# Exponent scaling of weight pieces on VectorE, shorter scratch stores, and the first small weight sums moved into the first GEMM

## The chip, the cores and the metric

The kernel runs on one core of a Trainium2 chip. The time is the device time of one execution in microseconds (us); before the change the median of four runs is 647.11 us (645.83 to 647.81). The engines are named as in the profile: PE is TensorE (PEld its weight loads), DVE is VectorE, ACT is ScalarE, POOL is GpSimd, and SP is SyncE, whose queue issues every DMA of this kernel.

## What is computed

A retention layer is followed by a two-layer network with ELU. All tensors are fp32; the weights reach the kernel as float64.

```python
# q, k, v: (4, 8, 768, 64);  w_in: (512, 2048);  w_out: (2048, 512)
gamma = 1.0 - 2.0 ** (-5.0 - np.arange(H))
for t in range(S):
    state = gamma * state + einsum('bhd,bhe->bhde', k[:, :, t], v[:, :, t])
    y[:, :, t] = scale * einsum('bhd,bhde->bhe', q[:, :, t], state)
x = y.transpose(0, 2, 1, 3).reshape(3072, 512)
h = x @ w_in
g = np.where(h > 0, h, np.exp(np.minimum(h, 0)) - 1)
out = g @ w_out
```

## The kernel before

The 3072 tokens are worked through in six blocks of 512. For each block the retention gives x (in chunks of 128 tokens), the first GEMM gives h, ELU gives g, and the second GEMM gives the output. From the second block on the GEMMs use Strassen's scheme, from there on partly twice nested. It replaces one of eight block products by sums of blocks of the weights and of the inputs. The sums of the weights are made once, in the first two blocks, and most of them are stored in DRAM (scratch, scratch2, scratch3) and fetched again later through a ring of buffers. The change lies in block 0 and in the making of these sums.

**Pieces.** The weights come as float64 in 16 pieces of 1 MB: pieces 0 to 7 are w_in, 8 to 15 w_out. `load_piece` (L136) loads one into one of three staging buffers (tile wraw). `prepare` runs three ScalarE operations on it: the low words scaled (L157), the exponent's top byte (L159), and the high words scaled by 2^-112 (L160). `decode` then runs two VectorE operations, a shift with a mask (L179) and an integer add (L182), which give the fp32 weights. Behind them it issues the load of the piece three further on, into the buffer just freed, and, for a piece of w_out, a store of the decoded blocks to scratch (L186). SP's queue is in order, so a load that waits for a decode holds up the DMAs behind it.

**Block 0, first GEMM (`plain_first`).** It is a plain product of 16 tiles (n = 0 to 15 in the loop at the end of the listing); a tile with 512 columns takes TensorE 3.4 us (L473). After each tile `elu` puts two activations on ScalarE (L440, L441) and one operation on VectorE (L444), which is put off to the next tile. Only L444 frees the tile's PSUM bank, and four banks go round. Between the tiles the loop emits other work by hand: loads of q, k, v for block 1 (`load`), their scaling on GpSimd (`scale_v`, L268), pieces (`next_piece`), and at n = 10 to 14 the retention of block 1: score products (L294) with masks on VectorE (L305), state products (L325) with state sums (L337), and the products of the outputs (L363, L389) with the copies `seen` (L377) and the scaling (L398). These products share four PSUM banks, in turn, so that each group of products needs the VectorE operations of the one before it to have read its bank.

**Block 0, second GEMM (`second_of_first`).** It has eight steps of seven products (L561), 6 us each. A step needs one decoded piece of w_out, four sums of its blocks (`sums_of_pieces`, L513, tile so), and four sums of the activations (`inputs_of_first`, L492). In its loop the kernel also makes the small sums, those of the nested scheme: `small_of_pieces` runs four operations on pieces of w_out and four on the sums (L597, in `combine_w_out`). Its results lie in xb (the x of block 0) and in gq["T3"] (named gT by the profile) until `send_small` stores them to scratch2 (L593). At the end the step's last products are added up on VectorE (`kept_sum`, L545), which frees the banks that the next GEMM begins with. `combine_x_parts(1)` (L417) writes the sums of block 1's x into xb.

**Block 1, first GEMM (`first`).** `combine_w_in` (L623) makes the sums of w_in. `combine_small` (L764) makes two nested sets of w_in on GpSimd, four operations each, near the end of this GEMM, and stores them to scratch3. Then the staging buffers are given up and the ring of fetched weights starts in their place.

The order on every engine is the order in which this program emits its instructions; each engine runs its own in order.

Of the kernel before, what the change touches and what calls it, by code (L numbers as in the profile page):

```python
# [9 lines left out]
FP32 = mybir.dt.float32  # L10
# [3 lines left out]
AF = mybir.ActivationFunctionType  # L14
# [4 lines left out]
def kernel(  # L19
# [119 lines left out]

    def prepare(parts=1):

        n = len(prepared)
        if n >= NPIECE:
            return
        t = staged[n]
        if n < 2 * NQ:
            dst = (w_a, w_b)[n % 2][n // 2].rearrange("p a b c d -> p (a b c d)")
        else:  # L150

            dst = w_s[n % NQ].rearrange("p a b c d -> p (a b c d)")[:, 0:1024]
        todo = []
        for part in range(parts):
            c = slice(part * 1024 // parts, (part + 1) * 1024 // parts)
            lo, hi, flat = t[:, c, 0], t[:, c, 1], dst.bitcast(U32)[:, c]
            nc.scalar.activation(flat, lo, AF.Copy, scale=2.0**-29)  # L157
            top = dst.bitcast(F8).rearrange("p (c b) -> p c b", b=4)[:, c, 3]
            nc.scalar.activation(top, hi.bitcast(FP32), AF.Copy, scale=2.0**-120, saturate=False)  # L159
            nc.scalar.activation(lo.bitcast(FP32), hi.bitcast(FP32), AF.Abs, scale=2.0**-112)  # L160
            todo.append((lo, flat))
        prepared.append((dst, todo))


# [1 line left out]


    quarters = lambda f: scratch.rearrange("(s k) p (f c) -> k f p s c", k=2, f=4)[f // 4, f % 4]

    def decode(fine=False):  # L170

        n = len(decoded)
        if n >= NPIECE:
            return
        dst, todo = prepared[n]
        decoded.append(dst.rearrange("p (a b) -> p a b", a=2))
        vec = nc.vector
        for c, flat in todo:
            vec.tensor_scalar(c, c, 3, 0x7FFFFFF8, ALU.logical_shift_left, ALU.bitwise_and)  # L179
            if fine:  # L180
                yield
            vec.tensor_tensor(out=flat, in0=c, in1=flat, op=ALU.add)  # L182
            yield
        load_piece()
        if n >= 2 * NQ:
            nc.sync.dma_start(quarters(ORDER_F[n - 2 * NQ])[:, 0:8], dst.rearrange("p (s c) -> p s c", c=P))  # L186

    def decode_all():
        for _ in decode():
            pass  # L190
# [316 lines left out]
    def sums_of_pieces(n):  # L507

        odd = n // 2 % 2
        t = so_[:, :, 3:7] if odd else so_[:, :, 0:4]  # L510
        both = w_s_.rearrange("p n j a b c -> p n (j a b c)")[:, n % NQ : n % NQ + 2, 0:1024]
        a21, a11, a12, a22 = (both[:, :, 256 * d : 256 * d + 256] for d in range(4))
        tt = lambda o, x, y, op: nc.vector.tensor_tensor(out=o, in0=x, in1=y, op=op)  # L513
        s4, s1, s2, s3 = (t[:, :, k] for k in range(4))
        tt(s1, a21, a22, ALU.add)
        tt(s2, s1, a11, ALU.subtract)
        for x in range(2):
            sums[n + x] = t[:, x]
        if odd:
            tt(s3, a11, a21, ALU.subtract)  # L520
            yield
            tt(s4, a12, s2, ALU.subtract)
        else:
            tt(s4, a12, s2, ALU.subtract)
            yield
            tt(s3, a11, a21, ALU.subtract)
        for x in range(2):
            nc.sync.dma_start(quarters(ORDER_F[n + x])[:, 8:16], sums[n + x].rearrange("p a (d c) -> p (a d) c", c=P))

    def small_of_pieces(at):  # L530

# [59 lines left out]
    def send_small():  # L591
        while to_send:
            nc.sync.dma_start(*to_send.pop(0))  # L593

    def combine_w_out(at, low, high):

        tt = lambda o, x, y, op: nc.vector.tensor_tensor(out=o, in0=x, in1=y, op=op)  # L597
        if at < 3:

            ms = [xb[:, k].rearrange("p (b c) -> p b c", c=P)[:, 0:3] for k in range(4)]  # L600
            ss = gq["T3"].rearrange("p (k f) (b c) -> p k (f b) c", k=4, c=P)
        else:
            ms, ss = (stage.tile([P, 4, 4, P], FP32, name="wi", tag="stage") for _ in range(2))
            ms = [ms[:, k, 0:3] for k in range(4)]
        ss = [ss[:, k] for k in range(4)]
        for first, dst, k in [(0, ms, 0), (3, ss, 1)][:: 1 if at < 3 else -1]:
            a11, a21, a12, a22 = (x[k][:, :, P * d : P * d + P] for x in (low, high) for d in range(2))
            s1, s2, s3, s4 = dst
            tt(s1, a21, a22, ALU.add)
            yield  # L610
            tt(s2, s1, a11, ALU.subtract)
            yield
            tt(s3, a11, a21, ALU.subtract)
            yield
            tt(s4, a12, s2, ALU.subtract)
            to = scratch2[first : first + dst[0].shape[1]].rearrange("j p (k f c) -> k f p j c", k=4, f=4)
            for k in range(4):
                to_send.append((to[k, at], dst[k]))
            yield
# [136 lines left out]

    W_IN = {2: w_a_[:, :, :, 1], 3: w_s_[:, :, 2]}

    def combine_small(j):

        t = stage.tile([P, 4, 4, P], FP32, name="wi", tag="stage")
        a11, a12, a21, a22 = (W_IN[j][:, 2 * r : 2 * r + 2, :, c, :] for r in range(2) for c in range(2))
        s1, s2, s3, s4 = (t[:, k].rearrange("p (n f) c -> p n f c", f=2) for k in range(4))
        tt = lambda o, x, y, op: nc.gpsimd.tensor_tensor(out=o, in0=x, in1=y, op=op)  # L764
        tt(s1, a21, a22, ALU.add)
        tt(s2, s1, a11, ALU.subtract)
        tt(s3, a11, a21, ALU.subtract)
        tt(s4, a12, s2, ALU.subtract)
        to_send.append((scratch3[j - 1], t.rearrange("p k f d -> p (k f d)")))
# [333 lines left out]
    def run(steps):  # L1103
        for _ in steps:
            pass

    def next_piece():
        decode_all()
        prepare()

    hslot = lambda: hpool.tile([P, 2, TH], FP32, name="h", tag="h")
    mslot = lambda: mpool.tile([P, 2, TH], FP32, name="m", tag="m")

    for n, _ in enumerate(inner):
        if n in (0, 2, 4, 6):
            load(CPB + n // 2)
        if n in (1, 3, 5, 7, 9):
            next_piece()
        if n in (3, 5, 7, 9):
            scale_v(CPB + (n - 3) // 2)  # L1120
        if n == 7:
            run(inputs_of_first(0, [hslot() for _ in range(3)]))
        elif n == 10:
            scores(1, 0)
            scores(1, 1)
        elif n == 11:
            decode_all()
            states(1, 0)
            states(1, 1)
            prepare()  # L1130
        elif n == 12:
            parts = inputs_of_first(4, [mslot() for _ in range(3)])
            next(parts)
            outputs_step(1, 0)
            prepare()
        elif n == 13:
            decode_all()
            outputs_step(1, 1)
            prepare()
            run(parts)  # L1140
        elif n == 14:
            decode_all()
            parts = sums_of_pieces(0)
            next(parts)
            outputs_step(1, 2)
        elif n == 15:
            run(parts)
            decode_all()

    for n in second_of_first():  # L1150
        send_small()
        if n == 0:
            run(small_of_pieces(0))
            prepare()
            parts = sums_of_pieces(2)
            next(parts)
        elif n == 1:
            run(parts)
            run(small_of_pieces(1))
            next_piece()  # L1160
        elif n == 2:
            next_piece()
            parts = sums_of_pieces(4)
            next(parts)
        elif n == 3:
            run(inputs_of_first(2, [hslot(), hslot(), mslot()]))
            run(parts)
            next_piece()
        elif n == 4:
            run(inputs_of_first(6, [hslot(), mslot(), hslot()]))  # L1170
            decode_all()
            parts = sums_of_pieces(6)
            next(parts)
        elif n == 5:
            run(small_of_pieces(2))
            run(parts)
        elif n == 6:
            run(combine_w_in(0))
            send_small()
            xparts = combine_x_parts(1)  # L1180
            next(xparts)
            next(xparts)
            held["last"] = small_of_pieces(3)
            for _ in itertools.islice(held["last"], 3):
                pass
    run(xparts)

    ring = tpool = None
# [17 lines left out]
    sides = [  # L1206
        itertools.chain(combine_w_in(1), last), itertools.chain(combine_w_in(2), combine_w_in(3)), iter(()), iter(()),
    ]
    smalls = [], [], [3], [2]
    for n in range(NQ):  # L1210
        load(2 * CPB + n)
        cur = first(n)
# [185 lines left out]
```

## Time and profile before

| What | us |
|---|---|
| median of the runs | 647.11 |
| profiled execution, its own time | 644.94 |
| its span (first to last instruction) | 642.9 |
| TensorE busy in the span | 628.4 |
| VectorE busy | 479.5 |
| ScalarE busy | 258.9 |
| GpSimd busy | 38.5 |
| block 0, first GEMM, from its first tile on | 17 to 87 |
| block 0, second GEMM | 87 to 138 |
| block 1, first GEMM | 142 to 194 |

The span is what the instructions cover; the execution's own time is 2.0 us longer. A line of the timeline gives the start, the length (for several instructions, that of all of them together), engine, line, operation, what is written and read, shapes and count, and in brackets how long the engine had been idle before it and what ended that. A line of the waits gives who waited for whom, the sum in us, the times, and the longest.

### The profile page before, as it was taken

Reading aid. Unit: us, or ns where it says so; the run is one execution under the profiler, and the core shown is the slowest. Engines: PE = TensorE matmul, PEld = TensorE weight load, DVE = VectorE, ACT = ScalarE, POOL = GpSimd, SP = SyncE. Lnnn points to the kernel's source line nnn. Section 1 sums busy time; section 2 is a strip of 40 time slices with the busy share of each in tenths; the row PEclk is TensorE's granted clock in tenths of the full one; section 3 lists DMA queues with packets and bytes.
Section 4 is the critical chain, followed back from the end, with each engine's and each line's share of the span. In section 5 each row is a group of like instructions: output and inputs, shape, how many; then the busy total and the mean of one; then the engine's idle time right before and its main releaser. Section 6 shows DMA issues by size and latency. Waiting matters only on the chain.

```text
span 642.9 us, 16071 instructions
## 1 busy us (share of the span) xinstructions
PE 628.4 (98%) x6622; PEld 561.5 (87%) x6622; DVE 479.5 (75%) x858; ACT 258.9 (40%) x480; POOL 38.5 (6%) x41
## 2 busy tenths in 40 slices
PE   7999999879999999999999999999999999999998
PEld 4764578768888999989999989999988999988997
DVE  5648797977978776589777488867578959557976
ACT  6789744204452112546111465211465311356311
POOL 1011000000450000100000110000020000000000
PEclk9999999999999999999999999999999999999999
DMA  8697699979387789802889821788840688710794
GB/s 308 283 325 273 200 274 275 317 218 244 142 273 241 237 253 319 282 2 68 253 278 291 295 82 30 219 282 274 290 171 3 197 269 274 219 45 1 213 314 161
DMA packets 84696, 139.72 MB, mean 217 GB/s; under 512 B 6672, under 2 KB 37776, under 8 KB 82320
## 3 DMA queue, kind: packets, MB, share of 16 engines
q1 hardware_dynamic: 84624, 138.70, 67.1%
q8 instruction: 52, 0.85, 0.5%
q14 instruction: 20, 0.16, 0.1%
HBM read 114.56 MB, written 24.12 MB: 216 GB/s over the span
## 4 chain that ended last, share of the span: by engine, by line
PE 75%; DVE 2%; DMA 1%; issue 1%; SPq 1%; ACT 0%; DVEq 0%
PE pa L898 20%; PE pa L859 10%; PE pd L898 9%; PE pb L898 5%; PE pa L813 5%; PE pb L859 4%; PE pa L689 4%; PE qa L859 3%; PE pd L813 2%; PE qd L859 2%; PE pd L859 2%; PE pd L689 1%; PE y L363 1%; PE sc L294 1%; PE y L389 1%; PE kv L325 1%
## 5 line engine op out<-in xcount | busy, mean ns | idle before, releaser
L906 ACT COPY ms<-pa 128x128 f32<-128x128 f32 x104 | 27.6, 265 | 146.9 <-PE pa L898 145.4
L898 PE MATMUL pa<-ts,wq 128*128 128x128 f32 x560 | 74.1, 275 | 0.3 <-ACT ms L906 0.3
L898 PE MATMUL pd<-ts,wq 128*128 128x128 f32 x552 | 73.2, 276 | 0.0
L898 PEld LDWEIGHTS pa<-ts,wq 128*128 128x128 f32 x560 | 68.6, 192 | 0.8 <-ACT ms L906 0.5
L898 PEld LDWEIGHTS pd<-ts,wq 128*128 128x128 f32 x552 | 67.2, 192 | 0.3 <-DVE res L910 0.2
L898 PE MATMUL pa<-gC,wq 128*128 128x128 f32 x480 | 64.7, 278 | 0.0
L441 ACT ACTIVATE r<-r 128x512 f32<-128x512 f32 x96 | 60.5, 630 | 3.0
L898 PEld LDWEIGHTS pa<-gC,wq 128*128 128x128 f32 x480 | 59.1, 192 | 1.3
L440 ACT ACTIVATE r<-gC 128x512 f32<-128x512 f32 x64 | 39.9, 624 | 33.3 <-DVE gC L867 33.3
L910 DVE TENSOR_TENSOR res<-pd,ms 128x128 f32<-128x128 f32 x68 | 19.4, 286 | 38.2 <-PE pd L898 37.0
L444 DVE SCALAR_TENSOR_TENSOR gC<-r,gC 128x512 f32<-128x512 f32 x64 | 45.4, 741 | 0.7 <-ACT r L441 0.7
L268 POOL TENSOR_TENSOR kvn<-kvn,vf 128x512 f32<-128x512 f32 x21 | 24.4, 1165 | 315.2 <-DMA kvn<-in_qkv_dram 233.0
L775 DVE TENSOR_TENSOR ts<-gC,ts 128x512 f32<-128x512 f32 x60 | 41.3, 688 | 1.0
L775 DVE TENSOR_TENSOR ts<-gC 128x512 f32<-128x512 f32 x60 | 40.9, 682 | 0.0
L898 PE MATMUL pb<-gC,wq 128*128 128x128 f32 x240 | 32.8, 277 | 0.1
L931 ACT COPY res<-pa 128x128 f32<-128x128 f32 x34 | 9.0, 265 | 56.2 <-PE pa L898 54.7
L898 PEld LDWEIGHTS pb<-gC,wq 128*128 128x128 f32 x240 | 29.5, 192 | 0.8 <-DVE gC L444 0.8
L639 ACT COPY m<-pa 128x512 f32<-128x512 f32 x24 | 13.9, 580 | 34.8 <-PE pa L689 21.7
L867 DVE TENSOR_TENSOR gC<-qa,gC 128x512 f32<-128x512 f32 x8 | 5.5, 691 | 25.1 <-PE qa L859 18.3
L859 PE MATMUL pa<-xt,w_b 128*128 128x256 f32 x96 | 23.0, 383 | 0.0
L859 PE MATMUL pa<-xt,w_s 128*128 128x256 f32 x96 | 23.0, 383 | 0.0
L859 PE MATMUL pa<-xb,w_a 128*128 128x256 f32 x96 | 22.7, 379 | 0.0
(253 smaller groups left out, 1258.2 us busy)
## 6 DMA issues: line engine op xcount, KB each, us to landing
wq<-scratch_dram SPq DMA_DIRECT2D x277, 256.0 KB, 4.4
wraw<-in_w_dram SPq DMA_DIRECT2D x16, 1024.0 KB, 6.3
qk<-in_qkv_dram SPq DMA_DIRECT2D x24, 512.0 KB, 7.1
kvn<-in_qkv_dram SPq DMA_DIRECT2D x24, 512.0 KB, 7.8
scratch_dram<-w_s SPq DMA_DIRECT2D x8, 512.0 KB, 7.1
scratch_dram<-so SPq DMA_DIRECT2D x8, 512.0 KB, 5.4
out_dram<-res SPq DMA_DIRECT2D x14, 256.0 KB, 4.1
scratch_dram<-gT SPq DMA_DIRECT2D x12, 256.0 KB, 4.4
```

What stands on the lines that cost most here:

```text
L268: eng.tensor_tensor(out=kv[:, 1], in0=kv[:, 1], in1=vf[:, i].unsqueeze(2).to_broadcast([C, H, D]), op=ALU.mult)
L440: nc.scalar.activation(e, h, AF.Relu, scale=-1.0)
L441: nc.scalar.activation(e, e, AF.Exp, scale=-1.0)
L444: nc.vector.scalar_tensor_tensor(g, e, -1.0, h, ALU.add, ALU.max)
L639: nc.scalar.copy(m, ps)
L689: nc.tensor.matmul(ps[:, fi, :], lhsT=w[:, fi, j2, :], rhs=x[:, j2, :], start=(begin and fi == 0 and j2 == 0), stop=(j2 == 1), skip_group_ ...
L775: sub = lambda o, x, y: nc.vector.tensor_tensor(out=o, in0=x, in1=y, op=ALU.subtract)
L813: nc.tensor.matmul(ps[:, f, :], lhsT=lhs[f], rhs=xs[j][k], start=(begin and f == 0), stop=True, skip_group_check=True,)
L859: nc.tensor.matmul(ps[:, fi, :], lhsT=w[:, fi, j2, :], rhs=x[:, j2, :], start=(j in (1, 7) and fi == 0 and j2 == 0), stop=(j2 == 1), skip_ ...
L898: nc.tensor.matmul(ps, lhsT=w[:, f, :], rhs=ts[j][k][:, f, :], start=(begin and f == 0), stop=(f == 3), skip_group_check=True,)
L906: nc.scalar.copy(m, ps)
L910: nc.vector.tensor_tensor(out=o, in0=x, in1=y, op=ALU.add)
```

## The change

It does five things.

- `prepare(by_vector=True)` leaves out the third ScalarE operation of a piece (L160), and `decode` does that scaling on VectorE, as a multiplication ahead of the shift. The loop of the first GEMM asks for it in all its calls; later pieces are prepared as before.
- In the first GEMM the pieces are decoded at n = 1, 2, 4, 5, 7, 8, 9, 11, 13 instead of 1, 3, 5, 7, 9, 11, 13, 14, 15.
- The stores of w_out's blocks to scratch leave out blocks that nobody reads: for four of the eight pieces every second block, and for all pieces the first two.
- `sums_of_pieces(0)` and `small_of_pieces(0)` move into the first GEMM (n = 10 to 15), `inputs_of_first(4)` from there into the first step of the second GEMM, and `inputs_of_first(0)` from n = 7 to n = 6. The small sums of w_out now lie in buffers of mpool instead of xb, and some of the activations' sums in xb instead of mpool.
- `combine_small(2)`, one nested set of w_in on GpSimd, moves from the end of block 1's first GEMM to n = 6 of block 0's, with gq["T3"] as its buffer; its store is issued at n = 8.

```diff
-            nc.scalar.activation(lo.bitcast(FP32), hi.bitcast(FP32), AF.Abs, scale=2.0**-112)
-            todo.append((lo, flat))
+            if not by_vector:
+                nc.scalar.activation(lo.bitcast(FP32), hi.bitcast(FP32), AF.Copy, scale=2.0**-112)
+            todo.append((lo, flat, hi if by_vector else None))
...
+    used = lambda f, a, b: slice(a, b, 2 if f < NF // 2 else 1)
...
-        for c, flat in todo:
+        for c, flat, hi in todo:
+            if hi is not None:
+                vec.tensor_scalar(c.bitcast(FP32), hi.bitcast(FP32), 2.0**-112, None, ALU.mult)
             vec.tensor_scalar(c, c, 3, 0x7FFFFFF8, ALU.logical_shift_left, ALU.bitwise_and)
...
-            nc.sync.dma_start(quarters(ORDER_F[n - 2 * NQ])[:, 0:8], dst.rearrange("p (s c) -> p s c", c=P))
+            f = ORDER_F[n - 2 * NQ]
+            nc.sync.dma_start(quarters(f)[:, used(f, 2, 8)], dst.rearrange("p (s c) -> p s c", c=P)[:, used(f, 2, 8)])
...
-            nc.sync.dma_start(quarters(ORDER_F[n + x])[:, 8:16], sums[n + x].rearrange("p a (d c) -> p (a d) c", c=P))
+            nc.sync.dma_start(quarters(f)[:, used(f, 8, 16)], of[:, used(f, 0, 8)])
...
-            ms = [xb[:, k].rearrange("p (b c) -> p b c", c=P)[:, 0:3] for k in range(4)]
+            ms = [mpool.tile([P, 2, TH], FP32, name="m", tag="m") for _ in range(4)]
...
-        if n in (1, 3, 5, 7, 9):
-            next_piece()
+        if n in (1, 2, 4, 5, 7, 8, 9):
+            next_piece(True)
...
-        if n == 7:
+        if n == 6:
+            combine_small(2, gq["T3"].rearrange("p (k f) (b c) -> p k (f b) c", k=4, c=P))
             run(inputs_of_first(0, [hslot() for _ in range(3)]))
+        elif n == 8:
+            send_small()
         elif n == 10:
             scores(1, 0)
             scores(1, 1)
+            parts = sums_of_pieces(0)
+            next(parts)
         elif n == 11:
             decode_all()
             states(1, 0)
             states(1, 1)
-            prepare()
+            prepare(by_vector=True)
+            run(parts)
         elif n == 12:
-            parts = inputs_of_first(4, [mslot() for _ in range(3)])
-            next(parts)
+            smalls = small_of_pieces(0)
+            some(smalls, 3)
             outputs_step(1, 0)
-            prepare()
...
         if n == 0:
-            run(small_of_pieces(0))
-            prepare()
+            run(inputs_of_first(4, [xslot(x) for x in range(3)]))
             parts = sums_of_pieces(2)
             next(parts)
+            prepare()
         elif n == 1:
+            smalls = small_of_pieces(1)
+            some(smalls, 4)
             run(parts)
-            run(small_of_pieces(1))
+            run(smalls)
             next_piece()
...
-            run(inputs_of_first(2, [hslot(), hslot(), mslot()]))
+            run(inputs_of_first(2, [hslot(), hslot(), xslot(3)]))
...
-            run(inputs_of_first(6, [hslot(), mslot(), hslot()]))
+            run(inputs_of_first(6, [hslot(), hslot(), xslot(0)]))
...
-    smalls = [], [], [3], [2]
+    smalls = [], [], [3], []
```

`some(steps, count)` runs the next `count` operations of a generator, and `xslot(n)` is a quarter of xb.

More of the change, by code (lines that the diff above doesn't have):

```diff
@@ L137, in load_piece, with prepare @@
             staged.append(t)
-    def prepare(parts=1):
+    def prepare(parts=1, by_vector=False):
         n = len(prepared)
@@ L527, in sums_of_pieces @@
         for x in range(2):
-            nc.sync.dma_start(quarters(ORDER_F[n + x])[:, 8:16], sums[n + x].rearrange("p a (d c) -> p (a d) c", c=P))
+            f = ORDER_F[n + x]
+            of = sums[n + x].rearrange("p a (d c) -> p (a d) c", c=P)
+            nc.sync.dma_start(quarters(f)[:, used(f, 8, 16)], of[:, used(f, 0, 8)])
     def small_of_pieces(at):
@@ L598, in combine_w_out @@
         if at < 3:
-            ms = [xb[:, k].rearrange("p (b c) -> p b c", c=P)[:, 0:3] for k in range(4)]
+            ms = [mpool.tile([P, 2, TH], FP32, name="m", tag="m") for _ in range(4)]
+            ms = [m.rearrange("p a (b c) -> p (a b) c", c=P)[:, 0:3] for m in ms]
             ss = gq["T3"].rearrange("p (k f) (b c) -> p k (f b) c", k=4, c=P)
@@ L757, with combine_small @@
     W_IN = {2: w_a_[:, :, :, 1], 3: w_s_[:, :, 2]}
-    def combine_small(j):
-        t = stage.tile([P, 4, 4, P], FP32, name="wi", tag="stage")
+    def combine_small(j, t=None):
+        if t is None:
+            t = stage.tile([P, 4, 4, P], FP32, name="wi", tag="stage")
         a11, a12, a21, a22 = (W_IN[j][:, 2 * r : 2 * r + 2, :, c, :] for r in range(2) for c in range(2))
@@ L1105, in run, with next_piece, some @@
             pass
-    def next_piece():
+    def next_piece(by_vector=False):
         decode_all()
-        prepare()
+        prepare(by_vector=by_vector)
     hslot = lambda: hpool.tile([P, 2, TH], FP32, name="h", tag="h")
-    mslot = lambda: mpool.tile([P, 2, TH], FP32, name="m", tag="m")
+    xslot = lambda n: xb[:, n].rearrange("p (a t) -> p a t", a=2)
+    def some(steps, count):
+        for _ in itertools.islice(steps, count):
+            pass
     for n, _ in enumerate(inner):
@@ L1138 @@
             outputs_step(1, 1)
-            prepare()
-            run(parts)
+            some(smalls, 2)
         elif n == 14:
-            decode_all()
-            parts = sums_of_pieces(0)
-            next(parts)
+            some(smalls, 2)
             outputs_step(1, 2)
         elif n == 15:
-            run(parts)
-            decode_all()
+            run(smalls)
     for n in second_of_first():
@@ L1152 @@
         if n == 0:
-            run(small_of_pieces(0))
-            prepare()
+            run(inputs_of_first(4, [xslot(x) for x in range(3)]))
             parts = sums_of_pieces(2)
             next(parts)
+            prepare()
         elif n == 1:
+            smalls = small_of_pieces(1)
+            some(smalls, 4)
             run(parts)
-            run(small_of_pieces(1))
+            run(smalls)
             next_piece()
@@ L1183 @@
             held["last"] = small_of_pieces(3)
-            for _ in itertools.islice(held["last"], 3):
-                pass
+            some(held["last"], 3)
     run(xparts)
```

## The prediction

> **What bounds the kernel now.** I read the page's busy shares, then TensorE's waits by stage, then each engine's timeline around them.
>
> ```profile
> PE 628.4 (98%) x6622; PEld 561.5 (87%) x6622; DVE 479.5 (75%) x858; ACT 258.9 (40%) x480; POOL 38.5 (6%) x41
> ```
>
> TensorE is idle for 642.9 - 628.4 = 14.5 us: 4.1 in the first 20 us and 2.9 behind the last matmul, which the change doesn't touch; the rest is small, except two waits in the second GEMM (87 to 142 us):
>
> ```profile
> PE pa L689 <- DVE m L545: 3.5, 1, 3.5
> PE x L561 <- DVE m L492: 2.3, 1, 2.3
> ```
>
> Both are waits for VectorE. The windows around them (length, PE, PEld, DVE, ACT, POOL busy, granted clock, DMA share, GB/s):
>
> ```profile
> 115.50:119.00 3.50, 3.47 (x16) 3.08 (x17) 3.43 (x5) 2.75 (x3) 0.00 (x0) 1.00 1.15 344
> 138.25:141.72 3.47, 0.00 (x1) 0.00 (x1) 3.38 (x6) 0.00 (x0) 0.00 (x0) 0.99 0.83 238
> 141.72:145.17 3.45, 3.45 (x8) 2.81 (x9) 3.28 (x6) 0.00 (x0) 0.00 (x0) 0.51 0.40 152
> 145.17:148.60 3.43, 3.43 (x17) 3.03 (x16) 2.57 (x5) 1.24 (x3) 0.00 (x0) 1.00 0.95 221
> ```
>
> After the wait of 3.47 the granted clock is 0.51 for 3.45 us, and TensorE does in it 8 matmuls where it does 17 in the next row: 1.7 us more. After the wait of 2.30 the clock stays 1.00. The two waits cost 2.30 + 3.47 + 1.73 = 7.5 us. VectorE's timeline shows why it is late:
>
> ```profile
> 99.90 0.56 DVE L597 TENSOR_TENSOR xb<-w_s 128x384 f32<-128x384 f32 x1 [1.67 <-DMA scratch_dram<-xb]
> 104.46 0.69 DVE L597 TENSOR_TENSOR gT<-gT,so 128x512 f32<-128x512 f32 x1 [1.36 <-DMA scratch_dram<-gT]
> 114.78 0.69 DVE L492 TENSOR_TENSOR m<-gC,h 128x512 f32<-128x512 f32 x1
> 137.12 0.69 DVE L417 TENSOR_TENSOR xb<-xt 128x512 f32<-128x512 f32 x1 [4.25 <-DMA scratch_dram<-xb]
> 140.98 1.48 DVE L545 TENSOR_TENSOR m<-pa,m 128x512 f32<-128x512 f32 x2
> ```
>
> Its queue is full from 87 us on, and where it stops, it waits for the store of a buffer that it wants to overwrite: 7.5 us with the small ones. The inputs that TensorE wants at 113.2 us are done at 115.5, the sum that frees a bank at 141.7.
>
> **What is taken out of the second GEMM.** small_of_pieces(0) leaves it: four operations of 0.55 and four of 0.68 with their gaps, 91.0 to 95.6, 4.6 us. inputs_of_first(4) comes in: four of 0.69, 2.8. The products now lie in mpool's buffers, and combine_x_parts writes the halves xb[1], xb[2], whose readers are long done: the wait of 4.25 has no cause left. small_of_pieces(0)'s stores start in the first GEMM, so that small_of_pieces(1) finds its buffers free: the other waits go too. From the last ELU of the first GEMM (ends 91.0) to the first kept sum (140.4) VectorE takes 49.4 us now, and then 49.4 - 7.5 - 4.6 + 2.8 = 40.1, with some 2 for ScalarE's preparation of pieces 13 to 15, which waits for TensorE's reads of w_s: 42.
>
> Late next there: the inputs of the fifth step would be done some 20 us after VectorE enters (2.8 + 2.1 + 2.2 + 0.7 + 2.7 + 1.9 + 1.5 wait + 1.9 + 2.1 + 2.8), at 112.3, where TensorE wants them at 116.3 (113.2 and the new stall below). The last kept sums now need the landing of small_of_pieces(2)'s stores (mpool and gT); sums and stores issued one after the other from 127 us land from 131.7 to 136.4 at 5 us each, the first GEMM's bank is free at 136, and TensorE comes at 138.25 - 2.3 + 3.1 = 139: 2 to 3 us of cover. I book the whole 7.5, between 4.5 (a DMA a few us later) and 7.5; a further gain has no place, TensorE being busy around.
>
> **Stores not made.** Sixteen of 512 KB become 4 x (192 + 384 + 256 + 512) = 5376 KB, 2816 less; at the 310 GB/s of that stretch 9 us of DMA time. No TensorE wait is put down to a DMA there; booked at nothing beyond the waits above (0 to 0.5).
>
> **combine_small(2)** leaves the time around 175 to 181 us. TensorE is busy there, and the first fetch of the ring (waits for that store, 184.9) lands at 187.7, before its use at 188.6: 0 to 0.3, booked 0.
>
> **What comes into the first GEMM.** I count eight by_vector calls, not nine. Each takes 1.1 us from ScalarE and gives VectorE a TENSOR_SCALAR of 128x1024 with the strides of the shift's:
>
> ```profile
> L179 DVE TENSOR_SCALAR wraw<-wraw x18: 418/689/1482, 10.7 to 120.7; 128x1024 uint32<-128x1024 uint32 x14, 128x512 uint32<-128x512 uint32 x4
> ```
>
> I take its 0.70; the other bound, one element at a time, comes from TENSOR_TENSOR at 128 and 512 elements (286 and 686 ns): 286 + 896 x 1.04 = 1.22 us. Less is excluded, an instruction is added. Decoding a piece then takes 0.70 + 0.70 + 1.15 = 2.55. combine_small(2) runs on GpSimd beside inputs_of_first(0). Its trace of now:
>
> ```profile
> 160.52 0.69 DVE L701 TENSOR_TENSOR gT<-gC,gC 128x512 f32<-128x512 f32 x1
> 172.14 0.68 DVE L644 TENSOR_TENSOR h<-pd,m 128x512 f32<-128x512 f32 x1
> 173.44 1.68 DVE L701 TENSOR_TENSOR gT<-gC,gC 128x512 f32<-128x512 f32 x1
> 174.54 1.71 POOL L764 TENSOR_TENSOR wi<-w_a 128x512 f32<-128x512 f32 x1
> 175.16 1.64 DVE L701 TENSOR_TENSOR gC<-gC,gC 128x512 f32<-128x512 f32 x1
> ```
>
> With both inputs in SBUF the operation takes 1.66 beside GpSimd instead of 0.69; with one in PSUM, 0.68. GpSimd needs 5.9 us for four, so inputs_of_first(0), 2.8 alone, takes about 5.8: 3.0 more. [...] Lower bound: nothing added, if the two hardly meet.
>
> VectorE's queue then. Piece 3 is decoded at 37.3 as now. Pieces 4, 5, 6 go through ScalarE's chain (ELU 1.2, two preparations 2.4) and are decoded at 41.3, 46.6 and 49.8. From there VectorE has no gap: six ELU ends at 0.60 (3.6), the inputs (5.8), pieces 7 to 10 at 2.55 (10.2), four masks of the scores (2.5), three of the first small sums (2.1), three state sums (1.3): 25.5, so 75.3. The y products (L363) reuse the PSUM banks which those state sums read, and TensorE is there at 72.2: **3.1 us of new stall**. A part of it falls earlier, at the kv products (66.5), which need the masks: about 1 and 2 us, with 3.4 us of a GEMM tile between. Before the change VectorE finished the state sums at 70.5, so this wait is new. Everything behind (small sums of piece 0, `seen` copies, xt) has its room: the two stalls move TensorE back as much, VectorE enters the second GEMM at 92.0 instead of 91.0.
>
> ScalarE's queue: a preparation waits for its piece's load, and the next ELU behind it. The DMA row:
>
> ```profile
> 34.00:60.00 26.00, 26.00 (x77) 14.26 (x76) 17.11 (x22) 25.09 (x33) 4.04 (x4) 1.00 0.97 353
> ```
>
> It is full. Pieces 6 to 12, four pairs of q/k/v and the 1 MB store of combine_small(2) are 12 MB, at 353 GB/s 36 us: to about 70. Piece 10 would be in at 65, prepared at 67.3, wanted by VectorE at 70.9; piece 11 at 68, wanted at 80. So hidden, by 3 us; at a rate a tenth lower it costs 1.7.
>
> SP's queue: each load waits for a decode; the store of combine_small(2) stands behind piece 11's load, small_of_pieces(0)'s stores behind piece 14's; nobody on the path waits for them.
>
> [...]
>
> **Sum.** -7.5 + 3.1 = -4.4. The profiled span 642.9 becomes 638.5, its run 644.94 becomes 640.5; the median of the runs is 2.17 above that run: 647.11 - 4.4 = **642.7**.
>
> **Rivals.**
> - Whole gain, 0.12: GpSimd and VectorE hardly meet, VectorE reaches the state sums at 72.3: -7.4, 639.7. For it: the shift beside GpSimd took only 1.02 to 1.48.
> - A rest of the stall at 138 stays, 0.14: the kept sums wait for the landings of mpool's and gT's stores (2 us later than I reckon, 1 to 3 us of idle): 644 to 646. For it: those stores took 3 to 5.4 us to land.
> - Slower, 0.26 for coming out at no gain or below, 0.18 for a measurable loss: VectorE is late at the state sums by more than was gained. The multiplication at 1.22 adds 2.1 over four pieces, GpSimd 0.9 (all four inputs at 1.66), the loads 1.7: 3.1 + 4.7 = 7.8, and in one piece the clock takes 1.7: +2.0, 649.1. It decides from a stall of 7.5, or 5.8 with the clock. Against it: three bad ends at once, or two and the clock.
> - Forecast, 0.48: 641.5 to 644.5.
>
> A measurement of this kernel tells 0.2%, 1.3 us, from no change. Faster: 0.48 + 0.12 + 0.10 of the second rival; same 0.12; slower 0.18. The range reaches from the whole gain, 639.7, to just past no change, 648.0.
>
> **What would show it.** No TensorE wait before L545 and L492 of this size, clock 1.00 after 138; a new wait of TensorE for VectorE near 67 and 72 to 75 us (L325, L363); L492 near 52 us at about 1.5 us; the multiplication at 0.70; L417 without a DMA wait. Wrong if ScalarE idles for wraw past 65 us with TensorE behind it, or if the multiplication shows 1.2.

## The result, and the profile after

The changed kernel takes 642.40 us (median of 38 runs, 640.63 to 645.97), the kernel before 646.26 us on the same chips (57 runs, 643.37 to 653.94). The ratio is 0.9935, with a 95% interval of 0.992 to 0.995: 3 to 5 us faster. Some executions lie over 1.5% above the fastest of their kernel; the ratios leave them out and the medians do not, which matters below for small2_late (three of its six runs, 649 to 652) and scalar_scale (six of 16).

The profiled execution has a span of 642.2 us and its own time is 644.02. The busy shares first:

```profile
PE 629.2 (98%) x6622; PEld 562.1 (88%) x6622; DVE 483.5 (75%) x866; ACT 251.2 (39%) x472; POOL 39.9 (6%) x41
```

VectorE has eight instructions more and ScalarE eight fewer: the multiplications. The waits of TensorE between 33 and 190 us (waiting line, releaser, us in total, times, longest):

```profile
PE kv L331 <- issue: 1.6, 1, 1.6
PE y L369 <- DVE kvn L343: 1.3, 1, 1.3
PE pa L479 <- DVE gC L450: 0.7, 1, 0.7
PE kv L331 <- DVE qk L311: 0.2, 1, 0.2
```

The two waits of before, 3.5 and 2.3 in the second GEMM, are gone. Behind them, at the first products of block 1, the granted clock is now 1.00, where it was 0.51 (columns as in the prediction's windows):

```profile
143.98:147.40 3.42, 3.42 (x17) 3.03 (x16) 2.73 (x5) 0.59 (x1) 0.00 (x0) 1.00 0.79 243
```

Four new waits lie in the first GEMM, 3.8 us in all. (L331 is L325 of before, L369 L363, L479 L473, L450 L444, L343 L337.) The line with "issue" names no releaser, but VectorE's timeline tells it: the kv products begin at 72.32 us, just behind the first of the four masks (L311), which free the PSUM bank that these products write. The masks and the output products of the kernel before, whose first tile with 512 columns begins at 40.18 us:

```profile
62.91 2.48 DVE L305 TENSOR_TENSOR qk<-sc,cmask 128x512 f32<-128x512 f32 x4
72.17 1.16 PE L363 MATMUL y<-qk,kvn 64*64 64x64 f32 x64
```

And of the changed kernel, where that tile begins at 43.39:

```profile
43.91 1.04 POOL L274 TENSOR_TENSOR kvn<-kvn,vf 128x512 f32<-128x512 f32 x1 [23.90 <-DMA kvn<-in_qkv_dram]
...
53.83 1.28 POOL L774 TENSOR_TENSOR gT<-w_a 128x512 f32<-128x512 f32 x1 [2.72 <-DVE w_a L187]
54.26 1.40 DVE L498 TENSOR_TENSOR h<-gC,gC 128x512 f32<-128x512 f32 x1
55.19 1.60 POOL L774 TENSOR_TENSOR gT<-gT,w_a 128x512 f32<-128x512 f32 x1
55.70 1.64 DVE L498 TENSOR_TENSOR gC<-gC 128x512 f32<-128x512 f32 x1
57.37 1.66 DVE L498 TENSOR_TENSOR h<-gC,gC 128x512 f32<-128x512 f32 x1
59.06 1.66 DVE L498 TENSOR_TENSOR h<-gC,h 128x512 f32<-128x512 f32 x1
...
61.24 0.94 DVE L183 TENSOR_SCALAR wraw<-wraw 128x1024 f32<-128x1024 f32 x1
...
68.23 0.69 DVE L183 TENSOR_SCALAR wraw<-wraw 128x1024 f32<-128x1024 f32 x1
...
71.53 2.48 DVE L311 TENSOR_TENSOR qk<-sc,cmask 128x512 f32<-128x512 f32 x4
...
80.19 1.55 PE L369 MATMUL y<-qk,kvn 64*64 64x64 f32 x62 [1.35 <-DVE kvn L343]
...
134.23 0.69 DVE L423 TENSOR_TENSOR xb<-xt 128x512 f32<-128x512 f32 x1
...
140.77 0.69 DVE L553 TENSOR_TENSOR gT<-x,m 128x512 f32<-128x512 f32 x1 [3.20 <-PE pa L569]
```

Here are the inputs at 1.4 to 1.66 us beside GpSimd's `combine_small` (L498), the new multiplication at 0.69 alone and at 0.94 beside GpSimd's scaling of v (L183), the masks and output products that come late, the write of xb that waited 4.25 us for a store and now waits for nothing (L423), and the kept sum, where it is now VectorE that waits 3.20 us for TensorE.

To compare executions I cut each trace at the same products. A: up to the first tile with 512 columns. B: from there to the second GEMM, with block 1's retention. C: the second GEMM, up to the first product of block 1. D: from there to the first product with a fetched weight. E: the rest. In us:

| | A | B | C | D | E | span |
|---|---|---|---|---|---|---|
| before | 40.18 | 46.98 | 54.55 | 46.87 | 454.32 | 642.9 |
| after | 43.39 | 52.24 | 48.35 | 45.12 | 453.15 | 642.2 |
| after, profiled again (after_again) | 40.27 | 52.20 | 48.35 | 45.12 | 452.94 | 638.9 |

So the change gives 6.20 in C and 1.75 in D, takes 5.25 in B, and nets 2.7. A and E differ by idle stretches of TensorE that come and go between executions: in A the first profile has one of 1.99 us, with a clock of 0.50 behind it (17.30 to 20.71 us), that the second has not (see the last section), and in E the kernel before has one of 1.07 us at 200 us; of the other profiles' E some have such a stretch and some have none. The fastest runs of the two kernels, 643.37 and 640.63, differ by 2.74, in the later measurement beside after_again by 3.46 (644.10 and 640.64).

### The profile page after: what moved, and what is told of

Its sections match the earlier page's. It is cut to its first block, busy times and chain, and to the rows that moved or that the text cites. A ratio compares the mean times of both kernels' runs of the same rounds, so it can differ in the third digit from the quotient of the medians.

```text
span 642.2 us, 16073 instructions
## 1 busy us (share of the span) xinstructions
PE 629.2 (98%) x6622; PEld 562.1 (88%) x6622; DVE 483.5 (75%) x866; ACT 251.2 (39%) x472; POOL 39.9 (6%) x41
## 4 chain that ended last, share of the span: by engine, by line
PE 88%; DVE 5%; DMA 3%; issue 2%; ACT 2%; POOL 0%; DVEq 0%
PE pa L908 20%; PE pa L869 10%; PE pd L908 10%; PE pb L908 5%; PE pa L823 5%; PE pb L869 4%; PE qa L869 3%; PE x L569 3%; PE pa L698 3%; PE pd L823 2%; PE qd L869 2%; PE pa L569 2%; PE pd L869 2%; PE y L369 2%; PE y L395 2%
## 5 line engine op out<-in xcount | busy, mean ns | idle before, releaser
L450 DVE SCALAR_TENSOR_TENSOR gC<-r,gC 128x512 f32<-128x512 f32 x64 | 44.9, 732 | 0.7 <-ACT r L447 0.7
L274 POOL TENSOR_TENSOR kvn<-kvn,vf 128x512 f32<-128x512 f32 x21 | 25.7, 1226 | 314.2 <-DMA kvn<-in_qkv_dram 223.0
```

Source lines behind the costliest of these rows:

```text
L274: eng.tensor_tensor(out=kv[:, 1], in0=kv[:, 1], in1=vf[:, i].unsqueeze(2).to_broadcast([C, H, D]), op=ALU.mult)
L450: nc.vector.scalar_tensor_tensor(g, e, -1.0, h, ALU.add, ALU.max)
```

## The experiments

Twelve runs; after_again is the changed kernel itself, and small2_late was run twice. Ratios are to the kernel before, measured together with it on the same chip; B, C and D are the stretches above.

| kernel | median (lowest) | ratio, 95% interval | B | C | D |
|---|---|---|---|---|---|
| after_again | 642.6 (640.64) | 0.9943 [0.9921, 0.9964] | 52.20 | 48.35 | 45.12 |
| small2_late | 645.3 (638.35) | 0.9891 [0.9845, 0.9937] | 57.64 | 48.35 | 45.12 |
| small2_late_again | 638.63 (638.18) | 0.9882 [0.9845, 0.9919] | 49.66 | 48.35 | 45.12 |
| states_first | 641.81 (639.89) | 0.9935 [0.991, 0.996] | 50.76 | 48.35 | 45.12 |
| late_and_first | 637.25 (636.73) | 0.9866 [0.9828, 0.9905] | 47.82 | 48.35 | 45.12 |
| late_and_first_scalar | 643.5 (638.64) | 0.9935 [0.9909, 0.996] | 51.08 | 48.35 | 45.13 |
| late_and_first_full | 637.88 (637.29) | 0.9864 [0.9829, 0.9899] | 48.40 | 48.35 | 45.12 |
| full_stores | 642.27 (640.91) | 0.9945 [0.9927, 0.9964] | 52.25 | 48.35 | 45.12 |
| before_short | 644.04 (641.65) | 0.9955 [0.9934, 0.9976] | 46.99 | 52.67 | 45.40 |
| scalar_scale | 646.16 (638.84) | 0.9955 [0.9923, 0.9987] | 51.41 | 48.35 | 45.12 |
| smalls0_back | 645.71 (643.27) | 0.9993 [0.9969, 1.0018] | 52.75 | 50.04 | 45.39 |
| before_small2_early | 651.14 (645.54) | 1.0062 [1.0041, 1.0083] | 51.53 | 56.16 | 45.42 |

My theory was that the second GEMM's two waits go because VectorE no longer stops there for stores, and that a part of it is lost again in the first GEMM because VectorE, beside GpSimd, is late for block 1's retention. Its rivals: the loss comes from the order of the work or from the loads; the gain comes from the shorter stores or from the scaling.

**after_again**, the changed kernel itself, unedited.

> The changed kernel once more, beside the runs below. My theory: no TensorE wait left before L553 and L498 in the second GEMM, a new stall of 3.8 us (0.65 before a tile of L479, 1.8 at the state products L331, 1.35 at the output products L369) in the first GEMM; ratio to before 0.993 to 0.994. The 2.0 us that TensorE stood at L395 at 17 us, ended by nothing in the profile, and the clock of 0.93 in the first 20 us are chance of that execution: absent or of another size here, with the first 512-column tile (L479) at about 40.2 us instead of 43.4. A rival: they come from the change (another order of the code), then they are here again and cost 3.2 us.

Span 638.9. The long stall in the start is not here, so the change does not bring it each time. B, C and D agree with the first profile within 0.04 us. One point of the theory did not come: the 1.35 us before L369 are not there. The granted clock was 0.50 from 70.9 to 74.3 us instead, and TensorE reaches L369 as late as the first time (36.88 us after the first 512-column tile, against 36.80).

**small2_late** and **small2_late_again** (one kernel; in the first profile TensorE stands for 5.05 us up to 84 us and the clock is 0.80 from 80 to 85 us and 0.51 from 85 to 90, so that B there is no measure): combine_small(2) goes back to block 1.

```diff
-            combine_small(2, gq["T3"].rearrange("p (k f) (b c) -> p k (f b) c", k=4, c=P))
...
-    smalls = [], [], [3], []
+    smalls = [], [], [3], [2]
```

> The changed kernel with combine_small(2) back at its old place near the end of block 1's first GEMM, nothing on GpSimd beside inputs_of_first(0). Theory: GpSimd's hold on VectorE (L498 at 1.66 instead of 0.69, L183 at 0.94) makes most of the lateness of 4 us at the state sums; without it the new stall shrinks. If only VectorE's queue counts, 4 us faster than the changed kernel (0.987 of before). If the loads take over as the limit (ScalarE waited 4.7 us for piece 10 at 69.3 us in the changed kernel's profile), only 1 to 2.5 us faster (0.990 to 0.992). Rival: the early start of the ring of fetched weights is what the change gains; then this is slower than the changed kernel by 1 us or more.

> The same kernel as small2_late, because its profiled execution was disturbed (a 5 us idle stretch of TensorE inside the first GEMM that had nothing to do with the edit). Theory 1: combine_small(2) on GpSimd slows VectorE's inputs from 0.69 to 1.66 us each, and this is what makes VectorE late for TensorE from the masks on; without it the stretch from the first 512-column tile to the second GEMM falls from 52.2 us in the changed kernel to 49 to 51 us (the wait for kvn 1.3 us goes, that for the masks shrinks below 0.8), the second GEMM stays at 48.35 and the ratio to the kernel before is 0.987 to 0.991. Rival: VectorE's lateness is the decode chain's own, from the late ELU ends; the stretch stays above 51.5 us with the waits at kv and y as they were, ratio 0.992 to 0.995.

The waits of TensorE in the second run:

```profile
PE y L369 <- DVE kvn L343: 1.4, 1, 1.4
PE kv L331 <- DVE qk L311: 0.2, 1, 0.2
```

B falls by 2.6 us, to 49.66, as the theory had it, and the ratio lies in its interval. But it is another wait that goes: the one before kv (1.6) and the one at L479 (0.7), while I had named that for kvn, which stays. C and D don't change, so that in its early place combine_small(2) costs 2.6 us and gives nothing.

**states_first**: the state products and sums come ahead of a piece's decode and of the first small sums.

```diff
             scores(1, 1)
-            parts = sums_of_pieces(0)
-            next(parts)
         elif n == 11:
-            decode_all()
             states(1, 0)
             states(1, 1)
+            decode_all()
+            parts = sums_of_pieces(0)
+            next(parts)
             prepare(by_vector=True)
```

> The changed kernel with the state sums of n = 11 ahead of the decoding of piece 10, and the first small sums (sums_of_pieces(0)) behind it: 2.1 + 2.6 us of VectorE's work moved from before the state sums to behind them. Theory: the stall at the output products (1.35 and some 0.4 of split products) goes, those at the tile and the state products (2.4) stay: 1.5 to 2 us faster than the changed kernel, 0.990 to 0.991 of before. If the stall isn't VectorE's queue but another wait (a load, ScalarE), the time stays within 0.5 us of the changed kernel.

```profile
PE kv L331 <- issue: 1.6, 1, 1.6
PE pa L479 <- DVE gC L450: 1.0, 1, 1.0
PE kv L331 <- DVE qk L311: 0.2, 1, 0.2
```

Now it is the wait for kvn (L369) that is gone; B is 1.44 shorter than in after_again. The two edits remove different waits. The ratio is not the expected one: 0.9935, beside 0.9943 for the changed kernel measured with it. So this edit alone is seen in the stretch and not in the time.

**late_and_first**: both edits.

> Both edits at once: combine_small(2) late, state sums ahead of the decoding. Theory: no stall of more than 0.5 us is left in the first GEMM, 4 to 5 us faster than the changed kernel, 0.986 to 0.987 of before. If the loads are the next limit, a wait of 1 to 1.5 us moves to the output products of n = 14 (L395, behind the copies `seen`), and the gain is 2 to 3.5 us (0.988 to 0.990).

```profile
PE kv L331 <- issue: 0.4, 1, 0.4
```

B is 47.82, within 0.84 us of before, with this one wait left. The median is 637.25: it beats both kernels, at 0.9866 of the kernel before. So the loss in B is made of VectorE's delay beside GpSimd (2.6 to 2.9 us) and of what the order puts ahead of the state sums (1.4 to 1.8); what the earlier places of the decodes may add is at most the 0.84 that is left.

**before_small2_early**: the kernel before, with combine_small(2) alone moved into the first GEMM; the inputs move from n = 7 to n = 9 to stand beside it.

```diff
-        if n == 7:
+        if n == 9:
+            combine_small(2, gq["T3"].rearrange("p (k f) (b c) -> p k (f b) c", k=4, c=P))
             run(inputs_of_first(0, [hslot() for _ in range(3)]))
...
         elif n == 13:
+            send_small()
...
-    smalls = [], [], [3], [2]
+    smalls = [], [], [3], []
```

> The kernel before with one part of the change alone: combine_small(2) on GpSimd inside the first GEMM, beside the inputs of first(0), which are moved from tile step 7 to 9 so that both run side by side; its store at step 13, nothing of it left in the second half. Theory: the inputs beside GpSimd take 1.66 us in place of 0.69 each, VectorE is 3 to 3.5 us later at the state sums, where it had 1.7 to 2.7 us to spare, so the first GEMM grows by 0 to 2 us and nothing is gained late: 0 to 1.5 us slower, ratio 1.000 to 1.003. Rival: the late combine_small(2) cost VectorE something there too, and it gains 1 us or more: ratio below 0.9985.

```profile
60.85 1.53 DVE L492 TENSOR_TENSOR h<-gC,gC 128x512 f32<-128x512 f32 x1
62.42 1.66 DVE L492 TENSOR_TENSOR gC<-gC 128x512 f32<-128x512 f32 x1
...
67.94 2.47 DVE L305 TENSOR_TENSOR qk<-sc,cmask 128x512 f32<-128x512 f32 x4
```

TensorE's wait for these masks, and the windows around it:

```profile
PE kv L325 <- DVE qk L305: 2.3, 2, 2.1
```

```profile
67.60:71.00 3.40, 2.02 (x85) 1.78 (x88) 3.40 (x7) 0.37 (x1) 0.95 (x1) 0.99 0.00 0
71.00:74.40 3.40, 3.40 (x43) 2.05 (x36) 3.30 (x7) 2.44 (x3) 0.00 (x0) 0.50 0.30 34
```

Slower by 4 us (2.6 to 5.4), more than either expectation. B grows by 4.55. TensorE waits 2.10 and 0.17 us for the masks, and then the granted clock is 0.50 for 3.4 us, of which no expectation spoke. I had looked at the slack of the state sums, and the masks, which had less, were late first. C and D together are 101.58 against 101.42: nothing is gained late here either.

**before_short**: the kernel before with the shorter stores alone (the diff's lines with `used`). **full_stores**: the changed kernel without them (`used` gives every block, and a piece's blocks are stored from 0 on). **late_and_first_full**: the same with late_and_first.

> The kernel before with only the shorter stores. VectorE's waits for landings of stores in the second GEMM (1.7 + 1.4 + 4.2 us) should shrink as 9 us of DMA time leave. Theory: the two stalls (2.3 and 3.5) shrink by 1 to 2.5 us together and[...] the 1.7 us of halved clock go too: 1.5 to 4 us faster than before (0.994 to 0.998). Rival: the shorter stores are all that the change gains: 0.9935. If stores don't matter at all: 1.000.

> The changed kernel with all blocks of w_out stored to scratch as before, 2816 KB more. Theory: no TensorE wait of the second GEMM hangs on a DMA once the products lie in mpool and xb is free, so 0 to 0.8 us slower than the changed kernel (0.993 to 0.995 of before); the last kept sums may wait some tenths for the landing of small_of_pieces(2)'s stores. Rival: the shorter stores are what takes the second GEMM's stalls away; then those stalls come back and it is 3 us or more slower (0.998 and above).

> The faster version with all of w_out's scratch stored, as the kernel before did. Theory: the decode's transfers are hidden once the small sums are early, as inside the changed kernel, so 0 to 0.8 us slower than late_and_first, second GEMM at 48.35 us, no wait of TensorE there: ratio 0.986 to 0.989. Rival: with the first GEMM's stalls gone everything comes 4 us earlier but the loads of pieces don't, so the stores (24 MB in place of 21 MB) are on the path again: 3 us or more slower, ratio above 0.990, a wait of TensorE or VectorE that ends with a DMA.

TensorE's waits in before_short:

```profile
PE pa L694 <- DVE m L550: 2.6, 1, 2.6
PE x L566 <- DVE m L495: 1.3, 1, 1.3
```

They were 3.5 and 2.3, and behind the wait of 2.6 the clock stays full (1.000 is its mean over the execution): C is 1.88 and D 1.47 shorter. Taken alone, the shorter stores are worth 3.35 us. VectorE still waits 5.3 of its 7.5 us for stores there (3.4 of them before `combine_x_parts`, L420). In full_stores C and D are those of the changed kernel. VectorE waits there for a store, ahead of its kept sum,

```profile
DVE gT L553 <- DMA scratch_dram<-gT: 3.9, 1, 3.9
```

but TensorE, which VectorE would otherwise wait for 3.2 us, is not late for it. Within the change the shorter stores therefore give nothing that is measured, and in late_and_first_full at most the 0.6 us by which B is longer (0.9864 against 0.9866 of another measurement): other parts of the change remove the same waits.

**smalls0_back**: `small_of_pieces(0)` goes back into the first step of the second GEMM.

> The changed kernel with small_of_pieces(0) back in the first step of the second GEMM (behind inputs_of_first(4)); its first-GEMM place came after the stall, so that stall stays as it is. Theory: VectorE ends the second GEMM 4.6 us later, against 2 to 3 us of cover: the first product of block 1 waits 1 to 2.5 us for L553 again, with full clock[...], 0.996 to 0.998 of before. Rival: freeing xb (the wait of 4.25 us) was all that counted; then no stall comes back and it equals the changed kernel, 0.9935.

```profile
PE pa L698 <- DVE m L553: 1.4, 1, 1.4
DVE gC L450 <- ACT r L447: 2.2, 1, 2.2
DVE gT L553 <- PE x L569: 2.2, 1, 2.2
```

The wait at the end of the second GEMM is back, with the size and the full clock that were expected (1.4 us, and a mean clock of 1.000); C grows by 1.69 and D by 0.27. The ratio, 0.9993, lies above the expected one (its interval reaches down to 0.997), with B 0.5 longer than in the changed kernel. But C and D together are still 6.0 us shorter than before, of the 7.95 of the whole change, and the two last lines, all of VectorE's waits from 93 to 145 us, name no store. So the early small sums are worth 2.0 us here, which is VectorE's time and not a wait for stores. Of the parts that bear on these waits, what this kernel and full_stores both keep is the new place of the buffers (small sums in mpool, sums of the activations in xb). That part was never run alone: the waits for stores that reached TensorE go when it is joined by either the early small sums or the shorter stores, and what it would do by itself stays open.

**scalar_scale**: the eight multiplications back on ScalarE (by_vector off). **late_and_first_scalar**: the same with late_and_first.

> The changed kernel with the exponent scaling of all pieces on ScalarE (by_vector off). It takes eight multiplications of 0.69 to 1.04 us off VectorE and puts eight activations of 1.1 us on ScalarE. Theory: pieces 4 to 9 follow each other through ScalarE's chain (1.2 for an ELU and then 3.5 instead of 2.4), so decoding comes later, and the ELU behind each preparation too: the stalls of the first GEMM grow by 0.5 to 1.5 us in sum, 0.994 to 0.996 of before. Rival: VectorE alone is the limit of the first GEMM; then 3 us less of its work before the state sums make it 2 to 3 us faster than the changed kernel (0.989).

> The faster version (combine_small(2) late, state sums ahead of the decode) with the eight exponent multiplications back on ScalarE. Theory: VectorE now has slack in the first GEMM, ScalarE's own chain (tanh and ELU pieces behind an exponent pair that is about 1.2 us longer each time) does not, so the wait of TensorE for gC near the first 128x512 tiles grows from below 0.7 to 1.5 to 2.5 us and the time is 1 to 2.5 us above late_and_first: ratio to the kernel before 0.988 to 0.991. Rival: scaling on VectorE buys nothing even here, as it bought nothing inside the changed kernel; within 0.5 us of late_and_first, 0.986 to 0.988.

In scalar_scale B is 0.8 us shorter than in the changed kernel; neither expectation had that. Two waits of TensorE are left:

```profile
PE pa L480 <- DVE gC L451: 2.3, 1, 2.3
PE y L370 <- DVE kvn L344: 0.6, 1, 0.6
```

The 0.7 at the tile has become 2.3, and the 1.8 before kv are gone. The time does not tell the two apart: the ratio is 0.9955, and 0.9945 for full_stores, whose stretches are the changed kernel's, in the same measurement. In late_and_first_scalar (its expectation speaks of tanh, which this kernel does not have; ScalarE's chain is ELU and the preparations) VectorE waits for ScalarE's third operation (L162):

```profile
63.24 1.48 DVE L185 TENSOR_SCALAR wraw<-wraw 128x1024 uint32<-128x1024 uint32 x1 [1.42 <-ACT wraw L162]
...
67.85 0.69 DVE L185 TENSOR_SCALAR wraw<-wraw 128x1024 uint32<-128x1024 uint32 x1 [1.28 <-ACT wraw L162]
```

With a third wait of 0.71 at 52.9 us that makes 3.4, and B is 3.3 us longer than in late_and_first. About half of that is the clock (an estimate: its mean over the execution is 0.995 where late_and_first has 1.000, and the kv products and the tile behind them take 3.50 and 4.24 us of TensorE, 2.51 and 3.70 there); TensorE's own waits grow from 0.4 to 2.1. The direction is the theory's, at more than its 1 to 2.5 us (the ratios differ by 4.5 us), and in another place (before kv, 1.8). So scaling on VectorE pays 3 us once VectorE has slack there; in the change as it stands VectorE has none, and the scaling gives nothing that is seen.

## Why the prediction was right

The sign, both places and the mechanism were right: VectorE's waits for stores left the second GEMM, and a part of that was lost because VectorE came late in the first. Two terms were mis-sized, and that the times agree within 0.3 us (642.4 for 642.7) is partly luck.

- **Second GEMM and its clock, -7.5.** Measured -6.20 (C) and -1.75 (D): -7.95. VectorE's waits for stores are gone and the clock is 1.00 behind its end (143.98 to 147.40). The cover of 2 to 3 us at the end was 3.2. The reasons were only in part those given: without the early small sums no store wait comes back (smalls0_back), so that `small_of_pieces(1)` finds its buffers free without them. They give 2.0 of the 7.95, shorter stores alone would have given 3.35, and the new buffers were not tried alone. (The ten terms up to the fifth step's inputs add up to 20.7 us, which makes 112.7 and not 112.3; nothing hangs on it.)
- **First GEMM, +3.1.** This is the mis-sized term: it measured +5.2. The output products (L369) begin 36.80 us after the first 512-column tile, and before they began 31.99 us after it: 4.8 later, and they then run another 0.4 longer because the sums come to them piece by piece. I had 3.1 at this place. The step was VectorE's gapless chain to the state sums. In the time of before (3.2 us taken off for the start) it begins at 50.5 instead of 49.8, and its third state sum ends at 77.3 instead of 75.3; the first output products go ahead at 77.0, when two of the sums are there, 1.7 later than I had. The inputs took 6.5 for my 5.8, and two of the multiplications, beside GpSimd, 0.94 where I had 0.70. GpSimd's 5.9 us for four operations is what the other nested set took in the trace of before (168.72 to 174.57); this set took 6.3 there (174.54 to 180.84). I also left out that a late L450 holds up the next tile: 0.7 of the waiting falls there.
- **GpSimd.** The row was the right size (1.66 an input): two-input operations in SBUF slowed from 0.69 to 1.66, and L450, with one input in PSUM, stayed at 0.68 in the same stretch (60.64). GpSimd is slowed too: an operation of this size takes it 1.04 alone (L274 at 43.91) and 1.60 to 1.74 beside VectorE. Both lie near the sum of the two times alone, 0.69 + 1.04 = 1.73. The price in this kernel is 2.6 us, for an early place that brings nothing.
- **combine_small(2) leaving the end, 0; shorter stores, 0 beyond the waits.** Both as measured (C and D of small2_late_again and of full_stores are unchanged).
- **Loads.** Piece 10 landed at 69.26, or 66.1 without the start's 3.2, for my 65. ScalarE idled 4.67 us for it, which was half of my sign of being wrong, but TensorE did not wait behind it: VectorE took the piece at 76.57 without a gap, so that the load was hidden, as reckoned.
- **Clock in the first GEMM, none.** That two stalls of 1 and 2 us leave the clock alone was my estimate, from the wait of 2.30 in the trace of before. It was 1.00 there in the first profile and 0.50 for 3.4 us in the second (70.9 to 74.3), with the same B (52.24 and 52.20).
- **The sum.** -7.95 + 5.25 = -2.7 is what the stretches show. The medians differ by 3.9 and the ratio says 4.2 (3.2 to 5.2), so that my -4.4 came close to the medians partly by luck: the runs of before spread more, with a median 2.9 above their lowest run where that of the changed kernel lies 1.8 above. The spread goes with the granted clock. Of the changed kernel's 38 runs 25 have a clock of 0.997 and a median of 641.7, and six have 0.992 and 645.0; no run of before that has its clock on record is above 0.997. Why before loses more is open. My 642.7 also started from 647.11, and before measured 646.26 beside the result.
- **Rivals.** The whole gain fell with the waits in B. A rest of the stall at 138 did not stay. The slower end would have needed 7.5 us of stall, or 5.8 with the clock; 5.2 came, so that it was nearer than I thought.

## What to carry to other kernels

Before work is put on GpSimd at an earlier time, look at what VectorE has to do beside it: here four GpSimd operations cost the kernel 2.6 us (4 in the kernel before, with a clock of 0.50 for 3.4 us) because VectorE's two-input operations went from 0.69 to 1.66 us, and leaving their old place gave nothing. When several edits of one change remove the same wait, what each seems worth depends on which others are there: the shorter stores gave 3.35 us alone and nothing beside the rest. Each has to be run alone and left out alone. Order a busy queue by who is waited for: three sums that TensorE needs, moved ahead of work that is due later, gave 1.4 us in the first GEMM.

## What the runs showed of the hardware

**After equal short idle stretches the clock was halved in one execution and full in another.** Waits of 2.30 (before) and 2.6 (before_short) between large products left it at 1.00. But after 1.59 and 0.22 us at the 64x64 products it was 0.50 in after_again. The windows of that trace (length, PE, PEld, DVE, ACT, POOL busy, clock, DMA share, GB/s):

```profile
67.50:70.90 3.40, 1.55 (x54) 1.25 (x53) 3.40 (x7) 3.16 (x5) 0.00 (x0) 0.99 1.02 365
70.90:74.30 3.40, 3.40 (x62) 2.62 (x63) 3.30 (x6) 1.53 (x3) 0.00 (x0) 0.50 1.01 406
```

The changed kernel's first profile has the same two waits and keeps 1.00:

```profile
68.50:71.90 3.40, 2.23 (x6) 0.68 (x4) 3.23 (x5) 2.58 (x3) 0.00 (x0) 1.00 0.93 265
71.90:75.30 3.40, 2.73 (x113) 2.42 (x114) 3.37 (x6) 2.26 (x5) 0.00 (x0) 1.00 1.02 389
```

Two more profiles keep a mean clock of 1.000 with such a pair at this place, 1.6 and 0.2 us in states_first and 2.0 and 0.2 in smalls0_back, and in before_small2_early the clock is 0.50 behind 2.10 and 0.17. So waits of this size cost clock here in some executions and none in others; what decides it is not shown. In the trace of before the clock is 1.00 from 5.13 us on, for 136.53 us, and then 0.50 for 3.41 (141.66 to 145.08); in the changed kernel's first it is 1.00 from 7.06 us on, for 10.24 us, and then 0.50 for 3.41 (17.30 to 20.71). The full stretches are 40 and 3 times as long as the halved ones.

**TensorE sometimes stops for nothing that the profile shows.** The stall at the start of the first profile:

```profile
17.14 0.27 PE L395 MATMUL pd<-qk,xt 64*64 64x64 f32 x1 [1.99 <-issue]
```

Such stretches came in four of the profiles at this line (1.4 to 2.3 us), and once as 5.05 us at 84 us in small2_late. The times of the instruction fetches (16 KB packets of queue q8) differ as well: between 9 and 20 us the profile above, with the stall, has one, at 14.3 to 15.7 us; that of before, without it, has one at 10.4 to 11.8 and one at 18.0 to 19.3. That the fetch is the cause was not tried. All four are profiles of kernels with the change, of which there are eleven; the three without it have none, which is too few to say that the change has no part in it. Such stretches are as large as what was to be measured here, so that the stretches between the same products decide and not one profile's span.
